# Attention followed by a gated feed-forward layer: where the matmul operands begin in a partition

## The chip, the cores and the metric

The kernel runs on one core of a Trainium2 chip. The metric is the time of one execution on the device, in microseconds (us). TensorE (PE) multiplies and transposes, PEld is its weight load, VectorE is DVE, ScalarE is ACT, GpSimd is POOL, and SyncE (SP) issues nearly all the DMAs. The on-chip memory has 128 partitions; a tile takes the same byte range in each of them. In the text, the offset of a tile is its first byte in the partition modulo 256.

## The reference

```python
scores = q @ k.T / sqrt(64) + bias     # 4 batches, 8 heads, 576 x 576; bias of log distances through a small net
attn = softmax(scores); a = attn @ v   # a: (4, 8, 576, 64)
x = a.transpose(0, 2, 1, 3).reshape(2304, 512)
h = x @ w_in                           # (2304, 2048)
g = s * relu(h) ** 2 + b
out = g @ w_out                        # (2304, 512)
```

All in fp32. The weights of the second part come as fp64 and are decoded on the chip.

## The kernel before

There are three stages. The first, to about 75 us, builds the bias in 36 steps. The second is attention: 16 pairs (a head and two batches), each in five row blocks, in a software pipeline (`step`, L476 on) that hands PE the scores of the block two ahead (L228), the transposes of the present block (L298 to L316) and the products of probabilities and values of the pair before (L332, L335). While it runs, `fill` slips in the decoding of the weights. The third is the feed-forward part, called the mixture here, from about 337 us to the end; its order is written out by hand in the last loop.

The mixture splits every operand into a high and a low fp32r part and multiplies three times (high by high, high by low, low by high). Tokens are taken in five chunks: 0 to 3 of 512 tokens, 4 of 256. The 2048 hidden columns are 16 blocks f, four to a group of weights g = 0..3. For a block, `expand(c, f)` does 12 matmuls (L429): the stationary operand is a 128 x 128 piece of `whi` or `wli` of the group, the moving one 512 columns of `x` (256 in chunk 4). ACT and DVE make `gt` of the result (L433 to L439). `project(c, f)` does three matmuls for each of four 128-token pieces (two in chunk 4), 12 in all (L453): stationary a piece of `gt`, moving 512 columns of `who` or `wlo`. PE gets expand(f), then project(f - 2), then expand(f + 1), and so on: one such pair of 24 matmuls is called a block below. In blocks of chunk 1 and later the projected f of the first two is the last two of the chunk before.

Two things depend on where tiles lie. Pools are laid out in the order they are made, from the left end or from the right end of a partition. The `x` of even chunks lies in pool `wraw` (which also takes the raw weights), that of odd chunks in `xp`; `wg0` holds group 0 of the weights, `wa` group 1, `w2` group 2, and `w30` and `w31` the two halves of group 3. Every slice that a matmul reads begins a multiple of 512 bytes into its tile, so it has the tile's offset. In `tp`, the tags `pr` (later `gt`), `tt` (later `r`), `vn` and `rb` lie one behind the other.

The second thing is `rt`, a row of softmax sums: once in a pair the sums are transposed, DVE copies them to `rt` (`norm_t`, L269 to L274), SP stores them with four small DMAs (`norm_store`, L278, L280), loads them back spread over 64 partitions into `rb` a block later (`norm_load`, L285), and DVE multiplies the result of the pair before by `rb` (L340). DVE works through its queue strictly in the order written.

Of the kernel before, what the change touches and what calls it, by code (L numbers as in the profile page):

```python
# [9 lines left out]
F32 = mybir.dt.float32  # L10
# [16 lines left out]
def attention_moe(ctx, tc, q, k, v, w_in, w_out, dist, par, out):  # L27
# [14 lines left out]
    LAST = 5 * NP  # L42

    const = ctx.enter_context(tc.tile_pool(name="const", bufs=1))
    wraw = ctx.enter_context(tc.tile_pool(name="wraw", bufs=2))
    dram = ctx.enter_context(tc.tile_pool(name="dram", bufs=1, space=DRAM))
    sm = ctx.enter_context(tc.tile_pool(name="sm", bufs=4))
    tp = ctx.enter_context(tc.tile_pool(name="tp", bufs=3))
    prep_ctx = ExitStack()
# [218 lines left out]

    def norm_t(p, ps):  # L269
        nc.tensor.transpose(ps[0:9, 128:256], rows.pop(p), ident)  # L270
        rt = sm.tile([9, 128], F32, tag="rt", name="rt", bufs=2)
        nc.vector.tensor_copy(rt, ps[0:9, 128:256])
        rts[p] = rt

# [12 lines left out]
    def probs_t(n, part):  # L287
# [8 lines left out]
        if t < 4 and part < 2:  # L296
            for kb in range(4):
                nc.tensor.transpose(  # L298
                    ps[:, 128 * kb:128 * kb + 128],
                    pr[:, part, 64 * part + 128 * kb:64 * part + 128 * kb + 128], ident)  # L300
            o, i = pt[:, :, part, c], ps.rearrange("p (a b) -> p a b", a=4)
            if part == 0:
                nc.scalar.activation(o, i, AF.Copy)
            else:
                nc.vector.tensor_copy(o, i)
        elif t < 4:
            nc.tensor.transpose(ps[:, 0:128], pr.rearrange("p x j -> p (x j)")[:, 512:640], ident)  # L307
            nc.scalar.activation(ptr[:, c], ps[:, 0:128], AF.Copy)  # L308
        elif part == 0:
            for kb in range(4):  # L310
                nc.tensor.transpose(  # L311
                    ps[:, 128 * kb:128 * kb + 128], pr[:, 0, 128 * kb:128 * kb + 128], ident)
            nc.vector.tensor_copy(
                pt[:, :, :, 512:S], ps.rearrange("p (a x b) -> p a x b", a=4, x=2))
        else:
            nc.tensor.transpose(ps[0:64, 0:128], pr[:, 0, 512:S], ident)  # L316
            for x in range(2):
                nc.scalar.activation(  # L318
                    ptr[64 * x:64 * x + 64, 512:S], ps[0:64, 64 * x:64 * x + 64], AF.Copy)
            norm_t(p, ps)  # L320
# [234 lines left out]
    for st in range(STEPS):  # L555
# [3 lines left out]
        for fn, *args in plan.get(st, ()):  # L559
            fn(*args)  # L560
    dctx.close()
    wg0 = ctx.enter_context(tc.tile_pool(name="wg0", bufs=1, side="right", reuse_waits="tile"))
    for kind in range(2):
        alloc_w(w_hi, kind, 0, wg0)
# [65 lines left out]
    for i in range(2, len(todo) + LAG):  # L630
        if i < len(todo):
            c, f = todo[i]
            if c == 0 and f in (6, 10):
# [3 lines left out]
                    name=f"w3{kind}", bufs=1, side=("left", "right")[kind], reuse_waits="tile"))  # L637
# [84 lines left out]
```

## Time and profile before

| | |
|---|---|
| Median of 3 runs | 747.52 us (746.73 to 747.52) |
| Span of the profiled execution | 747.1 us, 0.4 us under the median |
| PE busy | 716.6 us (96%) in 4530 matmul records |
| PE weight load busy | 534.9 us (72%) |
| DVE, ACT, POOL busy | 429.3, 363.5, 186.3 us |
| Granted TensorE clock, mean | 0.993 |
| Chain that ended last | PE 81%, issue 3%, POOL 3%, ACT 2%; by line L429 27%, L453 27% |
| Matmuls of the mixture | 960 in L429, 864 in L453 |

The span is the time from the first to the last instruction of the profiled execution; the runs were timed apart from it. Matmuls overlap in the records (one of 512 columns is shown with some 390 ns), so what one costs is read from start to start: a stretch of PE work divided by the number of matmuls that begin in it. The chain of waits gives such stretches directly, as pieces of so many matmuls of a line.

### The profile page before, as it was taken

The page shows a single profiled execution, that of the slowest core. Times are in us where ns is not written, and L with a number is a line of the kernel's source. Part 1 is how long each engine was busy: PE and PEld are TensorE (multiplying, and loading weights), DVE is VectorE, ACT ScalarE, POOL GpSimd, SP SyncE. Part 2 cuts the span into 40 slices and gives each one's busy share as a digit, 9 for nine tenths or more (in the row PEclk, how much of TensorE's full clock was granted, in tenths as well). Part 3 has the DMA queues.
Part 4 walks back from the last instruction along what each step waited for, and adds up shares of the span by engine and source line. Part 5 has one row for each costly group of instructions (what it writes and reads, how often), then busy time and mean ns, then how long its engine had stood idle before and what let it go on. Part 6 is the DMA issues. An engine that isn't in the chain of part 4 may idle for free.

```text
span 747.1 us, 12023 instructions
## 1 busy us (share of the span) xinstructions
PE 716.6 (96%) x4530; PEld 534.9 (72%) x4530; DVE 429.3 (57%) x794; ACT 363.5 (49%) x756; POOL 186.3 (25%) x194
## 2 busy tenths in 40 slices
PE   8978999899999999969999999999999999999998
PEld 4436666666666666646888888888888888888896
DVE  7976888788888878963288632233332332223332
ACT  7967767576666667653445322232222332222332
POOL 7991534445333234203654100000000000000000
PEclk9999999999999999989999999999999999999999
DMA  5977765556564765351012130000300002000100
GB/s 171 297 205 245 227 204 170 176 156 212 160 215 134 228 214 184 97 176 60 13 57 85 29 114 0 1 1 0 113 1 0 1 1 84 1 0 1 57 1 28
DMA packets 39817, 76.98 MB, mean 103 GB/s; under 512 B 9040, under 2 KB 12368, under 8 KB 39760
## 3 DMA queue, kind: packets, MB, share of 16 engines
q1 hardware_dynamic: 39616, 75.90, 32.4%
q8 instruction: 35, 0.57, 0.3%
q10 hardware_dynamic: 144, 0.33, 0.1%
q14 instruction: 22, 0.18, 0.1%
HBM read 55.45 MB, written 20.13 MB: 101 GB/s over the span
## 4 chain that ended last, share of the span: by engine, by line
PE 81%; issue 3%; POOL 3%; ACT 2%; DVE 1%; DMA 1%; SPq 1%; DVEq 0%; ACTq 0%; POOLq 0%
PE hps L429 27%; PE o L453 27%; PE sps L228 8%; PE xps L332 7%; PE tps L298 7%; PE xps L335 2%; PE tps L307 2%; PE tps L311 1%; POOL kr L204 1%; ACT ptr L318 1%; DMA x<-xt 1%; POOL qr L204 1%; PE tps L270 1%; POOL full L374 0%; PE tps L316 0%
## 5 line engine op out<-in xcount | busy, mean ns | idle before, releaser
L453 PE MATMUL o<-who,gt 128*128 128x512 f32 x576 | 192.5, 393 | 0.0
L429 PE MATMUL hps<-x,whi 128*128 128x512 f32 (+1 forms) x640 | 184.5, 373 | 0.0
L434 DVE SCALAR_TENSOR_TENSOR r<-r,sb 128x512 f32<-128x512 f32 (+1 forms) x80 | 56.7, 708 | 193.2 <-ACT r L433 193.2
L433 ACT ACTIVATE r<-hps 128x512 f32<-128x512 f32 (+1 forms) x80 | 44.4, 555 | 227.5 <-PE hps L429 227.5
L429 PEld LDWEIGHTS hps<-x,whi 128*128 128x128 f32 x640 | 117.5, 189 | 24.1 <-issue 0.4
L453 PEld LDWEIGHTS o<-who,gt 128*128 128x128 f32 x576 | 108.3, 188 | 24.1
L429 PE MATMUL hps<-x,wli 128*128 128x512 f32 (+1 forms) x320 | 119.0, 372 | 0.0
L253 ACT ACTIVATE pr<-tt,mn 128x576 f32<-128x576 f32 x144 | 110.1, 767 | 10.3 <-DVE mn L242 9.7
L453 PE MATMUL o<-wlo,gt 128*128 128x512 f32 x288 | 113.2, 393 | 0.0
L242 DVE CUSTOM_DVE_ANT_0 tt<-sps,bt 128x576 f32<-128x576 f32 x128 | 91.6, 753 | 29.4 <-PE sps L228 24.0
L228 PEld LDWEIGHTS sps<-kr,qr 64*128 64x128 f32 (+1 forms) x864 | 67.8, 185 | 39.6 <-issue 10.1
L228 PE MATMUL sps<-kr,qr 64*128 64x288 f32 (+1 forms) x864 | 88.3, 311 | 5.8 <-POOL kr L204 2.7
L439 DVE SCALAR_TENSOR_TENSOR gt<-r,sb,gt 128x512 fp32r<-128x512 f32 (+1 forms) x80 | 56.3, 704 | 54.0 <-ACT gt L438 54.0
L438 ACT ACTIVATE gt<-r,sb 128x512 fp32r<-128x512 f32 (+1 forms) x80 | 54.4, 680 | 52.2 <-DVE r L434 52.2
L298 PE MATMUL tps<-ident,pr 128*128 128x128 f32 x512 | 77.1, 282 | 0.3 <-ACT ptr L308 0.3
L332 PE MATMUL xps<-pt,vt 128*64 128x288 f32 x512 | 76.5, 421 | 0.0
L429 PEld LDWEIGHTS hps<-x,wli 128*128 128x128 f32 x320 | 60.3, 188 | 11.1
L298 PEld LDWEIGHTS tps<-ident,pr 128*128 128x128 f32 x512 | 57.7, 142 | 11.4 <-ACT ptr L308 11.2
L453 PEld LDWEIGHTS o<-wlo,gt 128*128 128x128 f32 x288 | 54.2, 188 | 11.6
L374 POOL TENSOR_SCALAR full<-full 128x512 f32<-128x512 f32 x32 | 22.6, 705 | 115.1 <-ACT full L372 114.6
L332 PEld LDWEIGHTS xps<-pt,vt 128*64 128x64 f32 x512 | 31.5, 137 | 24.3 <-issue 10.6
L136 PE MATMUL bps<-f,pt__110 128*32 128x512 f32 x288 | 42.8, 599 | 5.3 <-POOL f L119 2.2
(69 smaller groups left out, 748.1 us busy)
## 6 DMA issues: line engine op xcount, KB each, us to landing
bias<-stg SPq DMA_DIRECT2D x36, 288.0 KB
raw<-in_moe_w_in_dram SPq DMA_DIRECT2D x16, 512.0 KB
raw<-in_moe_w_out_dram SPq DMA_DIRECT2D x16, 512.0 KB
bt<-bias SPq DMA_DIRECT2D x7, 1152.0 KB
qt<-in_q_dram SPq DMA_DIRECT2D x16, 320.0 KB
kt<-in_k_dram SPq DMA_DIRECT2D x16, 320.0 KB
vt<-in_v_dram SPq DMA_DIRECT2D x16, 320.0 KB
rb<-rs SPq DMA_DIRECT2D x32, 144.0 KB
```

The costliest lines, as they stand in the source:

```text
L136: nc.tensor.matmul(pb[32 * c:32 * c + 32, 0:512], w2bd, fs[c][0][:, 0:8], start=True, stop=True)
L228: nc.tensor.matmul(o, a, b, start=(i == 0), stop=(i == 2))
L242: nc.vector.tensor_tensor_reduce(tt.rearrange("p (a b) -> p a b", a=2), ps[x][:, :, 0:HALF], bias.rearrange("p (a b) -> p a b", a=2), -1.0 ...
L253: nc.scalar.activation(pr[:, x], tts.pop((n, x)), AF.Exp, bias=mn[:, x:x + 1], scale=-1.0, accum_out=sums[p][:, col:col + 1])
L298: nc.tensor.transpose(ps[:, 128 * kb:128 * kb + 128], pr[:, part, 64 * part + 128 * kb:64 * part + 128 * kb + 128], ident)
L332: nc.tensor.matmul(ps[64 * x:64 * x + 64, hf, 0:HALF], vt[:, 4 * x + kb, :], pt[:, kb, x, c], start=(kb == 0), stop=False)
L429: nc.tensor.matmul(ps[:, 0:n], w[0, g][:, a, fc], xs_t[c, a][:, j, 0:n], start=(i == 0), stop=(i == 3 * KB - 1))
L433: nc.scalar.activation(r, ps[:, 0:n], AF.Relu)
L434: nc.vector.scalar_tensor_tensor(r, r, sb[:, 0:1], r, op0=ALU.mult, op1=ALU.mult)
L438: nc.scalar.activation(hi, r, AF.Identity, bias=sb[:, 1:2])
L439: nc.vector.scalar_tensor_tensor(lo, r, sb[:, 1:2], hi.bitcast(F32), op0=ALU.add, op1=ALU.subtract)
L453: nc.tensor.matmul(os_t[c][i], gt[:, a, tok], w[1, g][:, fo], start=(f == 0 and j == 0), stop=(f == NF - 1 and j == 2))
```

## The change

Three tiles that nobody reads or writes are put between pools, and `rt` has one buffer in place of two:

```diff
     const = ctx.enter_context(tc.tile_pool(name="const", bufs=1))
+    ctx.enter_context(tc.tile_pool(name="pad0", bufs=1)).tile([128, 32], F32, name="pad0")
     wraw = ctx.enter_context(tc.tile_pool(name="wraw", bufs=2))
     dram = ctx.enter_context(tc.tile_pool(name="dram", bufs=1, space=DRAM))
+    ctx.enter_context(tc.tile_pool(name="pad1", bufs=1)).tile([128, 32], F32, name="pad1")
     sm = ctx.enter_context(tc.tile_pool(name="sm", bufs=4))
...
-        rt = sm.tile([9, 128], F32, tag="rt", name="rt", bufs=2)
+        rt = sm.tile([9, 128], F32, tag="rt", name="rt", bufs=1)
...
     dctx.close()
+    ctx.enter_context(tc.tile_pool(name="pad2", bufs=1, side="right")).tile([128, 40], F32, name="pad2")
     wg0 = ctx.enter_context(tc.tile_pool(name="wg0", bufs=1, side="right", reuse_waits="tile"))
```

`pad0` and `pad1` take 128 bytes each on the left, `pad2` 160 on the right, and `rt` gives back 512. These offsets (bytes modulo 256) follow from the addresses in the two built programs:

| tile | before | after |
|---|---|---|
| `x` of chunks 0, 2 and 4 (and raw weights of groups 0 to 2) | 192 | 64 |
| `x` of chunks 1 and 3 | 64 | 64 |
| `gt` | 64 | 64 |
| weights of group 0 (`whi`, `wli`, `who`, `wlo`) | 224 | 64 |
| weights of groups 1 and 2; `whi`, `wli` of group 3 | 64 | 64 |
| `who`, `wlo` of group 3 | 224 | 64 |
| `pt`, `ptr` (transposed probabilities); `full` (decoded weights) | 224 | 64 |
| `q`, `k`, `v` tiles, their splits, `pr`, `tt`, `rb` | 64 | 64 |
| tiles of the bias stage (`f`, `stg`, `dst`, `ls`), `ident` | mixed | the same |

On all engines the instructions stand in the same order as before, and PE, ACT, POOL and SP wait for the same events. What differs is DVE's waits for DMAs, in 28 of its 799 instructions. This is the place of one pair's sums in DVE's queue, before; the names in brackets are what an instruction waits for, DMAHW0 to 7 being counters of landed DMAs:

```order
465 L272 COPY rt<-tps 9x128 [waits DMAHW5_49,PE_49]
466 L313 COPY pt<-tps 128x8x64 [waits PE_49]
467 L340 TENSOR_TENSOR rb<-xps,rb 128x576 [waits DMAHW1_49,DMAHW0_49,PE_49]
468 L382 SCALAR_TENSOR_TENSOR full_982<-raw,full_982 128x512 [waits DVE_49]
469 L242 ISA tt,mn<-sps,bt 128x576 [waits PE_49]
```

And the same place now (lines are two or three higher in the changed file):

```order
465 L274 COPY rt<-tps 9x128 [waits DMAHW5_49,DMAHW4_49,DMAHW6_49,DMAHW3_49,PE_49]
466 L315 COPY pt<-tps 128x8x64 [waits PE_49]
467 L342 TENSOR_TENSOR rb<-xps,rb 128x576 [waits DMAHW1_49,DMAHW0_49,PE_49]
468 L384 SCALAR_TENSOR_TENSOR full_994<-raw,full_994 128x512 [waits DVE_49]
469 L244 ISA tt,mn<-sps,bt 128x576 [waits PE_49]
```

Nothing moved; the copy to `rt` now waits for all four stores of the pair before (it overwrites what they read), where it waited for stores of the pair before that. Waits for a raw weight or for `rb` that this covers have gone from a few later instructions.

## Rows read from the trace of the kernel before

**Rows 1.** Busy time by stretch of the span: PE, PEld, DVE, ACT, POOL; then clock, DMA

```profile
core 0: us, PE busy (x) PEld busy (x) DVE busy (x) ACT busy (x) POOL busy (x), PEclk, DMA share, GB/s
345.00:428.00 83.00, 83.00 (x362) 66.60 (x361) 54.03 (x59) 38.10 (x66) 40.55 (x32) 1.00 0.15 47
428.00:516.00 88.00, 88.00 (x385) 72.05 (x384) 27.54 (x39) 24.20 (x38) 0.00 (x0) 1.00 0.08 24
516.00:602.00 86.00, 86.00 (x373) 69.71 (x372) 25.73 (x36) 22.67 (x36) 0.00 (x0) 1.00 0.08 25
602.00:690.00 88.00, 88.00 (x385) 72.06 (x384) 26.85 (x38) 23.46 (x39) 0.00 (x0) 1.00 0.06 19
```

**Rows 2.** Chain of waits, middle of chunk 1: start, us, what

```profile
471.66 2.72 PE hps L429 x12
474.38 2.72 PE o L453 x12
477.10 2.72 PE hps L429 x12
479.82 2.72 PE o L453 x12
```

**Rows 3.** Chain of waits, middle of chunk 2

```profile
565.60 2.79 PE hps L429 x12
568.39 2.73 PE o L453 x12
```

**Rows 4.** Chain of waits, blocks 1 and 2 of chunk 1 (weights of group 0)

```profile
432.87 2.80 PE hps L429 x12
...
441.27 2.81 PE o L453 x12
```

**Rows 5.** Chain of waits, end of chunk 3 (project with weights of group 3)

```profile
681.45 2.72 PE hps L429 x12
684.17 2.81 PE o L453 x12
```

**Rows 6.** PE busy by chunk, from one chunk's first matmul to the next one's

```profile
core 0: us, PE busy (x), PEclk, DMA share, GB/s
349.06:427.09 78.03, 78.03 (x338) 1.00 0.16 48
427.09:515.20 88.11, 88.11 (x385) 1.00 0.08 24
515.20:604.24 89.05, 89.05 (x385) 1.00 0.07 24
604.24:692.35 88.11, 88.11 (x385) 1.00 0.06 19
692.35:700.80 8.45, 8.45 (x49) 1.00 0.01 2
700.80:740.45 39.65, 39.65 (x253) 1.00 0.07 27
```

**Rows 7.** PE in order of time, expand(0, 1): start, us, what

```profile
344.65 0.40 PE L429 MATMUL hps<-x,wli 128*128 128x512 f32 x1
...
346.75 0.40 PE L429 MATMUL hps<-x,wli 128*128 128x512 f32 x1
```

**Rows 8.** Chain of waits, chunk 4

```profile
720.76 1.44 PE hps L429 x12
722.20 1.40 PE o L453 x6
```

**Rows 9.** Chain of waits, attention, one row block

```profile
275.08 1.00 PE sps L228 x12
276.08 0.26 PE tps L307
276.34 1.02 PE tps L298 x8
277.36 1.12 PE xps L332 x8
```

**Rows 10.** SP's queue in order of time: DMA issues

```profile
267.48 0.27 SPq L278 DMA_DIRECT2D rs<-rt  x1
268.34 0.23 SPq L280 DMA_DIRECT2D rs<-rt  x1
270.32 0.24 SPq L278 DMA_DIRECT2D rs<-rt  x1
271.05 0.21 SPq L280 DMA_DIRECT2D rs<-rt  x1
...
276.39 1.11 SPq L285 DMA_DIRECT2D rb<-rs  x2
```

**Rows 11.** DVE in order of time, the next copy to `rt`

```profile
280.87 0.27 DVE L272 COPY rt<-tps 9x128 f32<-9x128 f32 x1
281.07 0.67 DVE L313 COPY pt<-tps 128x512 f32<-128x512 f32 x1
281.96 0.76 DVE L340 TENSOR_TENSOR rb<-xps,rb 128x576 f32<-128x576 f32 x1 [0.22 <-PE xps L335]
```

**Rows 12.** Costliest groups: busy us, mean ns, idle before and what ended it

```profile
L340 DVE TENSOR_TENSOR rb<-xps,rb 128x576 f32<-128x576 f32 x16 | 12.1, 757 | 5.0 <-PE xps L335 4.1 <-DMA rb<-rs 0.7 <-DMA be<-bias 0.2
L272 DVE COPY rt<-tps 9x128 f32<-9x128 f32 x16 | 4.4, 274 | 0.1
```

## The prediction, made before the changed kernel was run

> **What bounds the kernel now.** I read the busy shares first, then the stretches of the span, then the chain of waits inside the mixture. In the mixture PE is busy in the whole of every stretch from 345 to 690 us at a granted clock of 1.00, so at the upper of its two levels, 2.4 GHz, while DVE and ACT are busy for a third of the time from chunk 1 on, and for 54 and 38 of 83 us in chunk 0 [rows 1]. Nothing but the pace of the matmuls sets the time there. So the next view is the chain, in which one piece is a run of 12 matmuls, and the reader is to compare pieces of the same line. In the middle of chunk 1 both lines take 2.72 us per 12 [rows 2], 226.7 ns for one. The same line L429 takes 2.79 in chunk 2 [rows 3] and 2.80 at the start of chunk 1 [rows 4]; L453 takes 2.81 at the start of chunk 1 [rows 4] and at the end of chunk 3 [rows 5], where L429 beside it takes 2.72. At 2.4 GHz, 512 columns are 213.3 ns: the quick matmul costs 544 clocks, 32 over its columns, the dear one 558 to 562.
>
> Laid beside the table of offsets, these pieces sort without an exception. Where stationary and moving operand both begin at 64, 12 matmuls take 2.72 (2.73 where dear ones came just before: L453 in chunk 2 [rows 3]). Where the moving operand is off, `x` at 192 [rows 3] or `who` and `wlo` at 224 [rows 5], they take 2.79 and 2.81. Where the stationary one is off, `whi` and `wli` of group 0 at 224 with `x` at 64 [rows 4], they take 2.80. It is not the time of the run that counts, nor what the other engines do: in chunk 2 slow L429 and quick L453 alternate every 2.8 us, and at the end of chunk 3 it is the other way round. Of group 3 the half at 64 is quick and the half at 224 slow, in the same blocks.
>
> **The change part by part.** *The mixture, chunks 0 to 3.* The three pads add no instruction; they put every weight, `x` and `gt` tile at 64. Then all pieces should be those of rows 2, and a block of 24 matmuls takes 2 x 2.72 = 5.44 us. From the third block to the first matmul of chunk 4 there are 62 blocks: 14 in chunk 0, 16 in each of the three others. They take now 78.03, 88.11, 89.05 and 88.11 us [rows 6]; at 5.44 they take 76.16, 87.04, 87.04 and 87.04. The gains are 1.87, 1.07, 2.01 and 1.07: 6.02 us. PE waits for nothing in these stretches, so all of it is on the path. What is late next would be DVE, ACT or POOL, which feed PE: in chunk 1 they already keep up with 5.44 a block [rows 2], and in chunk 0 the busiest has a third of its time free [rows 1].
>
> *Its edges.* The first two blocks of chunk 4 still project the end of chunk 3: two runs of 12 with `who` at 224, 2.81 each as in rows 5, become 2.72, 0.18 us. Expand(0, 0) and expand(0, 1) run between the last pieces of attention; in the latter, nine matmuls take 346.75 - 344.65 = 2.10 us, 233 ns each [rows 7], so there are 6.7 ns for each of those 24 that nothing else holds up: 0 to 0.16, of which I take 0.1.
>
> *Chunk 4.* Here 256 columns take 1.44 us per 12 [rows 8], 120 ns or 288 clocks: 32 over the columns, although `x` lies at 192. L453 takes 1.40 per 6, 233 ns, although `gt` and the weights of groups 1 and 2 both lie at 64. So offsets alone do not explain this chunk; alternating lengths may keep the reads out of step. The bounds: nothing, if the mixing does it, or 6 x 226.7 = 1.36 per run, 0.04 times some 16 runs, 0.6 us. The nearest row is nearer to nothing than to all; I take 0.2.
>
> *Attention.* `pt` and `ptr` move from 224 to 64 as moving operands of L332 and L335, true fp32 and two at a time. A block's eight records take 1.12 us [rows 9]. No row shows them at another offset. The nearest, rows 2 against rows 4, make 3.3%; on 64 such groups, 71.7 us, that is 2.4 us either way. I take nothing, because L332 reads its two halves 1152 bytes apart, so at 224 and at 96 now and at 64 and 192 then: one half was and will be off 64. The tiles of scores and transposes keep their offsets.
>
> *One `rt`.* Each of 15 copies now waits for the stores of the pair before. In the pair shown these are issued by 271.05 [rows 10]; the copy that waits starts at 280.87 [rows 11], 9.8 us later. Two places behind the copy in DVE's queue stands the product with `rb`, whose load from the same DRAM row is issued at 276.39, after the stores [rows 10], and which needs the stores landed and that load landed too. For this load DVE stood idle 0.7 us in all 16 pairs [rows 12]. So what the copy waits for has landed by then, and if the cover went, each us of lateness would hold the copy of `pt` and the product behind it, and PE with them. The waits also need three more instructions on DVE in all, bounded by the copy itself at 0.27 each: 0 to 0.8 us, hidden by DVE's idle time, so 0. The lost waits for raw weights gain nothing, since those stand behind work that had waited already.
>
> *Sum.* 6.02 + 0.18 + 0.1 + 0.2 = 6.5 us. The profiled span of 747.1 becomes 740.6; the runs' median lies 0.4 above the span, which gives 741.0.
>
> **A rule that speaks against it.** The Trainium skill, page "SBUF — State Buffer", section "Specifications (TRN2)", gives SBUF lines of 16 bytes, with a penalty for crossing into a new one. All offsets here are multiples of 32, so by that rule every operand crosses the same number of lines, and the change is worth nothing. Rows 2 to 5 show the same matmul at two prices, so something coarser than a 16-byte line counts; but the rule stands for the second case below.
>
> **The rivals.** *Nothing changes, 747.5 us.* The pieces could sort by where in memory a tile lies, not by its offset: all dear ones lie at the left end (`x` of even chunks) or in the rightmost quarter, and the pads shift them by 128 or 160 bytes only. For it speaks chunk 4, where an offset of 192 costs 256 columns nothing [rows 8]. Against it speak group 3, whose slow half begins some 10 KB beyond the end of its quick half [rows 5], and that two far ends would have to share a price that the middle has not. 7%.
>
> *Half locked, 742.9 us.* Rows 3 show 2.73 for a run of L453 that follows dear ones: it takes some matmuls to fall into step. If each handover between L429 and L453 broke the step, all 124 runs would lose 0.015 us, 1.9 us in all. Against it: rows 2 hand over at 2.72. 5%.
>
> *Attention moves by its bound, 738.6 or 743.4 us*, if L332 depends on `pt`'s offset as the mixture does. 5%, the two together.
>
> *Slower, about 756 us.* The stores of `rt` queue on SP behind transfers that wait for buffers; in the pair shown they already go out over 3.6 us [rows 10]. If they landed after the next copy is due, DVE would stop with the scores' reduction behind it and PE would run dry, once in each of 15 pairs. With 1 us each that is 15 us against the gain of 6.5. It decides from 0.43 us a pair on (6.5 / 15), so from a landing some 10 us after the issue. Against it stand the 0.7 us of rows 12. 3%.
>
> **How the numbers follow.** My forecast has 80%, the rivals 7, 5, 5 and 3%. The forecast's own range is its open terms (edges 0 to 0.16, chunk 4 from 0 to 0.6, 0 to 0.8 lost on DVE) and the 0.8 us by which the runs shown differ: 741.0 less 0.06, 0.4 and 0.8 is 739.7, and 741.0 with 0.1, 0.2, 0.8 and 0.8 is 742.9. Taking in attention's upper bound gives 739.7 to 743.4, which leaves out no change, slower, and attention's lower bound. What this measurement can tell from no change is 0.2%, 1.5 us. Faster by more: 80 + 5 + 5, so 0.90. Within: 0.07. Slower: 0.03.
>
> **What would show it.** In the changed profile's chain every run of 12 in chunks 0 to 3 takes 2.72 us, from the first full block on, with no difference between even and odd chunks; the 62 blocks take 337.3 us instead of 343.3. L332's piece stays at 1.12, and the copy to `rt` has no idle time before it. If `x` at 64 still gives 2.79 in chunk 2, or group 0 still 2.80, offsets are not the cause and the forecast falls; if PE shows idle time behind the copy to `rt`, the slower case has come.

## The result, and the profile after

The changed kernel takes 741.45 us (five runs, 741.06 to 741.87) against 747.33 before (five runs, 746.73 to 747.52; the 747.52 above is the median of the first three): 5.9 us less, a ratio of 0.9913 with a 95% interval from 0.9901 to 0.9926. Forecast were 741.0, and faster with 0.90.

The mixture by chunk, in the columns of [rows 6] and with its boundaries taken at the same matmuls:

```profile
core 0: us, PE busy (x), PEclk, DMA share, GB/s
347.34:423.76 76.42, 76.42 (x338) 1.00 0.16 49
423.76:510.80 87.04, 87.04 (x385) 1.00 0.08 25
510.80:597.84 87.04, 87.04 (x385) 1.00 0.08 25
597.84:684.88 87.04, 87.04 (x385) 1.00 0.06 19
684.88:693.24 8.36, 8.36 (x49) 1.00 0.01 2
693.24:732.72 39.48, 39.48 (x253) 1.00 0.07 27
```

Chunks 1, 2 and 3 take exactly 16 x 5.44 us; the even chunk 2, which had been the longest of them, is like its neighbours. The chain of waits in chunk 2, against [rows 3], and in chunk 4, against [rows 8]:

```profile
565.36 2.72 PE hps L431 x12
568.08 2.72 PE o L455 x12
...
715.96 1.43 PE hps L431 x12
717.40 1.39 PE o L455 x6
```

What else the forecast spoke of stays where it was: the piece of L332 (now L334) takes 1.12 us as in [rows 9], and the copy to `rt` follows its forerunner without a gap, as in [rows 11]; its group and that of the product with `rb` answer to [rows 12]:

```profile
282.57 1.12 PE xps L334 x8
```

```profile
279.24 0.08 DVE L244 DVE_READ_ACCUMULATOR2_ANT mn<- 128x1 f32 x1
279.24 0.27 DVE L274 COPY rt<-tps 9x128 f32<-9x128 f32 x1
```

```profile
L342 DVE TENSOR_TENSOR rb<-xps,rb 128x576 f32<-128x576 f32 x16 | 12.1, 758 | 4.9 <-PE xps L337 3.1 <-DMA raw<-in_moe_w_in_dram 1.2 <-DMA rb<-rs 0.6
L274 DVE COPY rt<-tps 9x128 f32<-9x128 f32 x16 | 4.4, 274 | 0.1
```

The profiled spans differ by more than the medians, 747.1 against 739.3. Of the 7.8 us between them, 1.8 lie before the mixture, almost all in one wait for a DMA at the end of the bias stage. DVE in order of time there, before and after:

```profile
67.31 0.76 DVE L242 CUSTOM_DVE_ANT_0 tt<-sps,be 128x576 f32<-128x576 f32 x1 [2.42 <-DMA be<-stg]
```

```profile
65.69 0.76 DVE L244 CUSTOM_DVE_ANT_0 tt<-sps,be 128x576 f32<-128x576 f32 x1 [0.87 <-ACT pr L255]
```

It is not the change's doing: the other executions below, among them the same kernel again, start the mixture (the first matmul of L431) anywhere from 334.3 to 336.9 us, in no order by their offsets.

### The profile page after: what moved, and what is told of

Same layout as the page of the kernel before. It is cut to its first block, busy times and chain, and to the rows that moved or that the text cites. A ratio compares the mean times of both kernels' runs of the same rounds, so it can differ in the third digit from the quotient of the medians.

```text
span 739.3 us, 12026 instructions
## 1 busy us (share of the span) xinstructions
PE 711.2 (96%) x4530; PEld 536.3 (73%) x4530; DVE 429.5 (58%) x794; ACT 363.1 (49%) x756; POOL 186.7 (25%) x194
## 4 chain that ended last, share of the span: by engine, by line
PE 80%; issue 3%; POOL 3%; DMA 2%; ACT 1%; DVE 1%; SPq 0%; POOLq 0%; ACTq 0%
PE hps L431 27%; PE o L455 27%; PE sps L230 8%; PE xps L334 7%; PE tps L300 7%; PE xps L337 2%; PE tps L309 1%; DMA rs<-rt 1%; PE tps L313 1%; POOL kr L206 1%; ACT ptr L320 1%; DMA x<-xt 1%; POOL qr L206 1%; PE tps L272 1%; PE tps L318 0%
## 5 line engine op out<-in xcount | busy, mean ns | idle before, releaser
L455 PE MATMUL o<-who,gt 128*128 128x512 f32 x576 | 190.2, 389 | 0.0
L431 PE MATMUL hps<-x,whi 128*128 128x512 f32 (+1 forms) x640 | 182.8, 370 | 0.0
L431 PEld LDWEIGHTS hps<-x,whi 128*128 128x128 f32 x640 | 117.6, 189 | 22.1 <-issue 0.4
L455 PEld LDWEIGHTS o<-who,gt 128*128 128x128 f32 x576 | 108.2, 188 | 22.1
L431 PE MATMUL hps<-x,wli 128*128 128x512 f32 (+1 forms) x320 | 118.0, 369 | 0.0
L455 PE MATMUL o<-wlo,gt 128*128 128x512 f32 x288 | 112.2, 390 | 0.0
L334 PE MATMUL xps<-pt,vt 128*64 128x288 f32 x512 | 76.6, 422 | 0.0
L431 PEld LDWEIGHTS hps<-x,wli 128*128 128x128 f32 x320 | 60.5, 189 | 10.0
L455 PEld LDWEIGHTS o<-wlo,gt 128*128 128x128 f32 x288 | 54.1, 188 | 10.7
L334 PEld LDWEIGHTS xps<-pt,vt 128*64 128x64 f32 x512 | 31.5, 137 | 24.3 <-issue 10.6
```

Source lines behind the costliest of these rows:

```text
L334: nc.tensor.matmul(ps[64 * x:64 * x + 64, hf, 0:HALF], vt[:, 4 * x + kb, :], pt[:, kb, x, c], start=(kb == 0), stop=False)
L431: nc.tensor.matmul(ps[:, 0:n], w[0, g][:, a, fc], xs_t[c, a][:, j, 0:n], start=(i == 0), stop=(i == 3 * KB - 1))
L455: nc.tensor.matmul(os_t[c][i], gt[:, a, tok], w[1, g][:, fo], start=(f == 0 and j == 0), stop=(f == NF - 1 and j == 2))
```

## The experiments

Theory A is that of the forecast, put more sharply: a matmul of 512 columns is cheap when its stationary and its moving operand have the same offset, and dear when they differ.

**One part undone: the row buffer.**

```diff
-        rt = sm.tile([9, 128], F32, tag="rt", name="rt", bufs=1)
+        rt = sm.tile([9, 128], F32, tag="rt", name="rt", bufs=2)
```

> The three pads stay, the row of softmax sums has two buffers again; every offset is that of the changed kernel (512 bytes more on the left are 0 modulo 256). Theory A, the offsets alone make the gain: 741.4 us as the changed kernel, every run of 12 matmuls in chunks 0 to 3 at 2.72 us. Rival, the single buffer has a part in it (a wait it adds or a wait it takes off later DVE instructions): the time differs from 741.4 by more than 0.5 us, either way, and the difference lies before the mixture, with the runs of 12 unchanged.

Measured: 741.83 us (741.35 to 742.55, ratio to before 0.992, 0.9907 to 0.9934), all runs of 12 in chunks 0 to 3 at 2.72 but for the first block:

```profile
565.64 2.72 PE hps L431 x12
```

So one buffer neither costs nor gains anything that this can tell; it only makes room.

**One part alone: `x`.** The changed kernel without its right pad:

```diff
-    ctx.enter_context(tc.tile_pool(name="pad2", bufs=1, side="right")).tile([128, 40], F32, name="pad2")
```

> Only the left pads: x of chunks 0, 2 and 4 goes from 192 to 64, weights of group 0 and who/wlo of group 3 stay at 224, pt stays at 224. Theory A (a matmul is dear when either operand is off the other's offset): chunks 0 and 2 become like chunk 1 of the kernel before, 88.11 us for chunk 2 instead of 89.05 and 76.9 for the 14 blocks of chunk 0 instead of 78.03, 2.1 us in all, so 745.2; L429 in the middle of chunk 2 2.72, L453 with group 3 still 2.81. Rival (one side's offset alone counts, the weights'): no gain, 747.3, chunk 2 as before.

Measured: 745.95 us (744.31 to 747.13, ratio 0.9977, 0.9966 to 0.9987). Chunk 2 takes 88.11 us (from 511.66 to 599.77) as forecast; in its middle all is cheap, at its end L455, whose weights of group 3 are still at 224, is dear beside cheap L431:

```profile
558.95 2.72 PE o L455 x12
...
588.87 2.72 PE hps L431 x12
591.59 2.81 PE o L455 x12
```

**The other part alone: the weights.** The kernel before with `pad2` and nothing else.

> Only the right pad, with two row buffers: weights of group 0, who/wlo of group 3, pt and ptr go from 224 to 64, x of even chunks stays at 192. Theory A: chunks 1 and 3 at 87.04 us (all runs 2.72), chunks 0 and 2 alternate 2.79 (L429) and 2.73 (L453), 88.4 for chunk 2 and 77.4 for the 14 blocks of chunk 0; 3.4 us and 0.2 at the edge less, 743.7. Rival (x alone counts): no gain. The two halves should add up to the whole 5.9 within 0.5 us.

Measured: 744.14 us (742.82 to 744.64, ratio 0.9948, 0.9935 to 0.996). Chunk 1 takes 87.04 us, chunk 2 88.43; its L429, with `x` at 192, is dear beside cheap L453:

```profile
562.58 2.79 PE hps L429 x12
565.38 2.73 PE o L453 x12
```

The totals were forecast 0.8 and 0.4 us lower. In the profiled executions chunk 0 is 0.6 us longer than forecast: its 14 blocks take 77.48 us with `x` alone (forecast 76.9) and 78.00 with the weights alone (77.4). Their first project waits for the last product with `rb`, and that for a load. The chain with `x` alone:

```profile
345.19 3.19 DMA rb<-rs
...
349.41 3.04 PE o L455 x12
```

The two halves save 1.8 and 3.6 us of the 747.73 that the kernel before took on that chip, 5.4 together; the whole saved 5.9. They add up within the scatter, and each did it in the pieces that its operands enter.

**Is 64 the good offset, or is it being the same?** All of the changed kernel's tiles at 192, and in another run at 96:

```diff
-    ctx.enter_context(tc.tile_pool(name="pad0", bufs=1)).tile([128, 32], F32, name="pad0")
...
-...name="pad2", bufs=1, side="right")).tile([128, 40], F32, name="pad2")
+...name="pad2", bufs=1, side="right")).tile([128, 8], F32, name="pad2")
```

```diff
+...name="pad0", bufs=1)).tile([128, 40], F32, name="pad0")
+...name="pad2", bufs=1, side="right")).tile([128, 32], F32, name="pad2")
```

> All tiles that the changed kernel has at 64 lie at 192 instead (weights, x, gt, and with them q, k, v, pr, pt). Theory A, stationary and moving operand must have the same offset, whichever it is: all runs of 12 at 2.72, 741.4 us. Rival B, 64 itself is the good offset (or a multiple of 256 plus 64): runs of 12 at 2.79 to 2.81 everywhere, some 124 runs x 0.08 = 10 us more than the changed kernel, 751.

> All tiles of the changed kernel moved from 64 to 96, an odd multiple of 32. Theory A: runs of 12 at 2.72, about 741.5 us. Rival D: a common offset serves only if it is a multiple of 64; runs of 12 at 2.79 or more, 751 us.

Measured: 742.10 us (739.73 to 742.85, ratio 0.9917, 0.9903 to 0.9932) at 192, and 742.06 in one run at 96. The chain in chunk 2, at 192 and at 96:

```profile
561.35 2.72 PE hps L430 x12
564.07 2.72 PE o L454 x12
```

```profile
560.88 2.72 PE hps L431 x12
563.60 2.72 PE o L455 x12
```

Rivals B and D fall: no offset is good by itself.

**How much may they differ?** Pads in front of each group's pool put the four groups of weights at four offsets, `x` and `gt` staying at 64. One of the added lines, the others being alike:

```diff
+    ctx.enter_context(tc.tile_pool(name="pad4", bufs=1)).tile([128, 16], F32, name="pad4")
     wa = ctx.enter_context(tc.tile_pool(name="wa", bufs=1, reuse_waits="tile"))
```

> x and gt stay at 64; the weights of groups 0, 1, 2, 3 begin at 96, 128, 192, 160, so 32, 64, 128 and 96 bytes off. Theory A (any difference costs the same): all runs of 12 in chunks 0 to 3 at 2.79 to 2.81, the 62 blocks at 5.60 to 5.62 each, 10 to 11 us more than the changed kernel, about 752. Rival C (the price grows with the difference, or comes only at some multiple): runs of some group stay at 2.72, or the four groups give clearly different lengths.

> As the run before with weights of groups 0 to 3 at 32, 0, 224, 64: 224, 192, 160 and 0 bytes above x and gt (32 and 64 below, for the first two). Theory A: groups 0, 1, 2 at 2.79 to 2.81, group 3 at 2.72 (2.73 after dear runs): about 749. Rival C: a difference of one sign or of 64 only is free, and its group is at 2.72 as well.

Measured: 750.78 and 749.51 us in one run each; the kernel before took 746.98 on that chip, the one at 96 742.06. The chain in chunk 2; of the first run a piece of L455 in groups 0 to 3 (moving weights at 96, 128, 192, 160; L431 takes 2.78 to 2.80 throughout):

```profile
530.20 2.80 PE o L455 x12
...
552.59 2.76 PE o L455 x12
...
580.38 2.78 PE o L455 x12
...
602.72 2.81 PE o L455 x12
```

Of the second, L431 in group 0 (at 32), the third and the fourth block of group 1 (at 0), and both lines in group 3 (at 64):

```profile
526.99 2.79 PE hps L431 x12
...
549.26 2.75 PE hps L431 x12
...
554.80 2.79 PE hps L431 x12
...
599.32 2.72 PE hps L431 x12
602.04 2.73 PE o L455 x12
```

Every difference costs here, and none gets under 2.72. But the price is not one: with the moving operand 64 bytes above the stationary one it is mostly 2.75 to 2.77, elsewhere 2.77 to 2.81. Nor does it hang on the two offsets alone: the four expands of group 1 in the second run have the same two offsets, yet the three that follow a project of group 0 take 2.75 and the fourth, which follows one of group 1, 2.79, in each of chunks 0 to 3. So rival C holds in its weak form, and the forecast of about 752 for the first run was 1 us too high.

**And by less than 32 bytes?** A row of spare columns in each weight tile lets the groups begin 4, 8, 16 and 48 bytes higher:

```diff
+        e = (1, 2, 4, 12)[g]
+        t = pool.tile([128, 2048 + 64], F32R, name=f"w{'hl'[parts is w_lo]}{'io'[kind]}{g}")
+        parts[kind, g] = t[:, e:e + 2048].rearrange("p (a b) -> p a b", a=4)
```

> x and gt at 64, the weights of groups 0, 1, 2, 3 begin 4, 8, 16 and 48 bytes higher, at 68, 72, 80 and 112. Theory A (any difference costs): all runs of 12 at 2.79 to 2.81, about 751. Rival E (only a coarser unit counts, 16 or 32 bytes): groups 0 and 1, or 0 to 2, at 2.72 and only the rest at 2.79 or more.

Measured: 749.59 us in one run. L457, with its moving weights 4, 8, 16 and 48 bytes above `gt`, chunk 2:

```profile
528.62 2.84 PE o L457 x12
...
551.08 2.80 PE o L457 x12
...
578.98 2.78 PE o L457 x12
...
601.29 2.80 PE o L457 x12
```

Rival E falls: one fp32 word already costs, and as a moving operand above the stationary one it is the dearest of all. But a difference is not always dear. Of the four expands of group 2 (`x` 16 bytes below the weights) three take 2.79 to 2.80 and the last 2.74, in each of chunks 0 to 3. The third and the fourth in chunk 2:

```profile
570.67 2.79 PE hps L433 x12
...
576.24 2.74 PE hps L433 x12
```

PE in order of time in the fourth: six matmuls in 1.36 us, 226.7 ns each, the pace of equal offsets.

```profile
576.78 0.62 PE L433 MATMUL hps<-x,whi 128*128 128x512 f32 x2
...
578.14 0.62 PE L433 MATMUL hps<-x,whi 128*128 128x512 f32 x2
```

This one follows a project of group 2, the three others projects of group 1. So theory A holds on one side only: in chunks 0 to 3 every run at equal offsets came into step, that is to 226.7 ns a matmul, and at different ones every run but this one of each chunk stayed out of it; what ran just before seems to have a part in that, which no run here tried by itself. The measure is 256 bytes, by the addresses in the built programs: in the kernel before, `gt` lies at 64 modulo 512 and the weights of group 1 at 320, and L453 is cheap with them [rows 2], while `x` and the weights 128 bytes apart are dear [rows 3].

**A further step: `x` of chunk 4 moved.** Chunk 4 does not fall into step at equal offsets; in the first run with shifted weights its 256-column matmuls were quicker with the moving operand 64 bytes below. So `x` of chunk 4 alone moves:

```diff
+    def shift(c):
+        return 48 if chunks[c][1] == 256 else 0
...
-                nc.tensor.matmul(ps[:, 0:n], w[0, g][:, a, fc], xs_t[c, a][:, j, 0:n],
+                nc.tensor.matmul(ps[:, 0:n], w[0, g][:, a, fc], xs_t[c, a][:, j, s:s + n],
```

> The changed kernel, with x of chunk 4 written and read 48 columns (192 bytes) further into its tile, at offset 0. In the two runs with shifted weights, matmuls of 256 columns took 115.2 ns where the moving operand lay 64 bytes below the stationary one and 119.4 at equal offsets. If that carries over, 192 matmuls save 4.2 ns each: expand in chunk 4 goes from 1.43 to 1.38 us per 12, a block there from 2.82 to 2.77, 0.8 us in all, 740.6 against 741.4. Rival: the gain of expand is given back by the matmuls of 512 columns that follow (project 1.39 to 1.43): no change.

> The changed kernel once more, beside the run with x of chunk 4 at offset 0, for the same chip: 741.4 us. Where the span differs from 739.3 by up to 2 us, the difference lies before the mixture starts, in the DMAs of the bias stage, and every run of 12 in chunks 0 to 3 is 2.72 us again.

Measured on the same chip: 741.52 us (739.97 to 744.49, ratio to before 0.9912, 0.9892 to 0.9932) and, for the changed kernel again, 743.14 (741.53 to 744.85, ratio 0.9935, 0.9918 to 0.9952). The forecasts were 740.6 and 741.4; on this chip the kernel before took 747.81. The changed kernel's six runs alone spread over 3.3 us, more than the effect; the stretch from chunk 4's first matmul to the last shows it, here with the shift and without:

```profile
686.74:736.72 49.98, 49.98 (x313) 1.00 0.06 22
```

```profile
685.35:736.07 50.72, 50.72 (x313) 1.00 0.06 21
```

0.74 us, close to the 0.8 forecast, but by another road: expand only goes from 1.43 to 1.41, where 1.38 was forecast, while project now locks at 6 x 226.7.

```profile
711.81 1.41 PE hps L435 x12
713.22 1.36 PE o L459 x6
```

So this version takes 0.74 us off the changed kernel in the stretch that it touches. Its median is the lower of the two, but the ranges overlap, so the run times alone do not show a gain.

## Why the prediction was right

*The cause.* The runs of 12 sort by equal offsets, as the forecast read from [rows 2 to 5]; the two halves alone, and the common offsets 192 and 96, show that it is the equality that brings the quick pace, and not a place in memory. The case of no change has fallen with it, and so has the half-locked one: from the third run of chunk 0 to the end of chunk 3, 2.72 is held through every handover. What spoke for no change, that 256 columns cost nothing more at 192 [rows 8], was true and meant something else: short matmuls have another order of prices (below).

By the 16-byte lines of the Trainium skill ("SBUF — State Buffer", section "Specifications (TRN2)") all operands that begin at a multiple of 16 bytes would cross the same number of lines, and the kernels before and after would be equal. The runs disagree: 2.72 against 2.79 to 2.81 in those two, and 2.78 and 2.80 at differences of 16 and 48 bytes. The forecast concluded from its rows that something coarser than such a line counts; what counts is the difference between the two operands, down to 4 bytes, which cost up to 10 ns a matmul.

*The 62 blocks.* Forecast 6.02 us; measured 343.29 to 337.54, 5.75. Chunks 1 to 3 are exact to 0.01. The term that was mis-sized is chunk 0, 76.42 where 76.16 stood. The missing 0.26 lies in its first block, which begins behind the last pieces of attention; from the third run on the chain has 2.72:

```profile
347.72 2.74 PE hps L431 x12
350.46 2.74 PE o L455 x12
353.20 2.72 PE hps L431 x12
```

Most of it was there before, and in the 78.03: the first run starts 0.38 us behind the first matmul now and 0.37 before, where that was at 349.06 [rows 6], against 0.16 at the start of chunk 1. The forecast counted this delay as a gain.

```profile
349.43 2.79 PE hps L429 x12
```

It scatters: with equal offsets chunk 0 takes 76.40 to 77.27 us in the profiled executions, 76.67 in the same kernel again.

*The edges.* Forecast 0.18 and 0.1, measured 0.09 (8.45 to 8.36) and nothing: a run of 512-column matmuls behind 256-column ones at equal offsets does not start in step (2.75), and the first two blocks wait between pieces of attention.

*Chunk 4.* Forecast 0.2 between bounds of 0 and 0.6; measured 0.17 (39.65 to 39.48).

*Attention and `rt`.* Taken at nothing, and nothing it was: 1.12 us a group, no wait at the copy, no difference with two buffers. For L332 that was luck, since the reason given was wrong. The `v` tiles lie at 64, so before the change both halves of `pt`, at 224 and 96, were off; now the first, at 64, matches and the second, at 192, does not. By the forecast's own 3.3% half of 71.7 us would have become quicker, 1.2 us in all. Nothing did: the piece takes 1.12 us in both kernels, and also in those with `pt` and `v` at 192 and at 96. So L332 shows no price for these offsets at all.

The slower rival rested on stores that land late; the group of L342 shows 0.6 us of waiting for what stands behind those stores, in 16 pairs. The margin was not wide. Where the chain goes through such a store, it takes 7.65 us, and the copy that must wait came 9.8 us after the issue [rows 10, 11]:

```profile
316.04 7.65 DMA rs<-rt
```

*The sum and its base.* Forecast 6.5 us, measured 5.9; the terms read from the two traces make 5.75 + 0.09 + 0.17, 6.0. One error lay under the sum: the profiled execution before was taken as a usual one, 0.4 us of time outside its span. The changed kernel's profiled execution took 741.06 us for a span of 739.3, 1.8 outside. So the execution profiled before was itself some 1.4 us above the median, which its late DMA at 67 us would explain. As the forecast subtracted from the median in the end, this did no harm.

## What to carry to other kernels

Where TensorE runs without a gap, measure matmuls from start to start by the tiles they read, and sort these by their first byte modulo 256: two prices for the same shape were a matter of layout here, and three unused tiles removed the dearer one at no cost that these runs can tell. For 512 columns put the stationary and the moving operand at the same offset; 64, 96 and 192 served alike. Where column counts alternate, try the shorter ones a little off, and look at what follows them, not at them alone.

## What was not expected of the hardware

A difference of one word (4 bytes), with the moving operand above, is the dearest seen: 2.84 us per 12 or 568 clocks a matmul against 544 at equality. The same two offsets can have two prices, it seems by what ran before: 2.75 and 2.79 with the moving operand 64 bytes above, 2.79 and 2.74 with it 16 bytes below. Matmuls of 256 columns mostly go the other way: at equal offsets they take 1.43 per 12, with up to 64 bytes between the operands 1.37 to 1.42, at 96 to 160 bytes 1.41 to 1.44. With the moving one 64 bytes below, 12 take 1.37 to 1.41 in the run with four offsets (group 1 in chunk 4), and 1.41 throughout where `x` of chunk 4 was moved:

```profile
708.91 1.41 PE hps L431 x12
...
711.72 1.37 PE hps L431 x12
```

None of the offsets tried brings a run of 512 columns under 544 clocks a matmul, 32 over the columns. What in the chip the two reads share, why the pace stays locked once it is in step, and why one kind of run fell into step at a difference, these runs do not show.
